# A recurrent attention loop: copies go from VectorE to GpSimd and ScalarE, two softmaxes behind the next query copy, and a load into the step

## The chip, the cores and the metric

The kernel runs on one core of a Trainium2 chip. A core has a matrix engine (TensorE, PE in the profile; its weight loads are PEld), VectorE (DVE), ScalarE (ACT), GpSimd (POOL), SyncE (SP, used here to start transfers) and 16 DMA engines that all transfers share. Each engine takes its instructions in the order in which the program gives them, and an instruction that has to wait holds up the ones behind it on that engine. The metric is the time of one execution in microseconds (us) of device time.

## The reference: what is computed

Two independent results lie side by side in the output. The first is a long convolution by FFT (1024 columns of 2048 rows); the change doesn't touch it. The second is a transformer layer with a memory that recurs over 64 segments of 32 rows:

```
mem = mem0                                   # 8 rows of 1024
for s in range(64):
    h = concat([mem, x[32 s : 32 s + 32]])   # 40 rows
    q, k, v = h Wq, h Wk, h Wv               # 32 heads of 128
    p = softmax(mask(q k^T * 128**-0.5))
    o = sum over heads of (p v) Wo           # 40 rows of 1024
    mem = o[:8];  out[32 s : 32 s + 32] = o[8:]
```

Segment s + 1 needs the 8 memory rows of segment s, so the 64 steps follow one another. A step uses all of Wq, Wk, Wv and Wo.

## The kernel before, in words

**Ahead of the loop.** The FFT convolution runs, and meanwhile everything that doesn't depend on the recurrence is computed for all segments: queries, keys and values of the last 8 rows of each segment (`QKBd`, `VBd` in DRAM). A step then works on 32 rows (8 of memory, 24 of x) and adds those 8 from the stored values.

**Weights.** They are cut into pairs of 512 KB. Most lie in SBUF for good (`Wqk`, `Wv`, `Wo`, `Wearly`); 17 pairs a step are read from DRAM through a ring of five buffers (`wring`, L713, started by SP), and two more are parked in PSUM and copied into ring buffers by ScalarE and VectorE (L719, L720). A ring buffer's next load starts when the matmuls that read it are done (`done`, which calls `place`).

**A step.** The 32 heads go in four units u0 to u3 of 8 heads. The order is written out by hand: a manual schedule puts each engine's instructions in the order of the Python calls in the loop over `s` (L906 on), and no scheduler moves them. The functions are:

- `qk_part` (L753): queries and keys of a unit, accumulated in PSUM over 8 weight pairs. `qk_out` (L759): ScalarE copies them to `qks`.
- `v_part` (L767), `v_out` (L774): the same for the values of two units, into `vsb`.
- `tr_a` (L780, L788 to L790): TensorE transposes `qks`; GpSimd puts the stored keys (`qkb`) and ScalarE the transposed queries and keys into `QK`.
- `scores` (L810 to L825): TensorE writes mask plus products into `S` in PSUM; VectorE takes the row maximum and subtracts it.
- `softmax` (L831 to L842): GpSimd clears part of `P`, ScalarE writes two exponentials into it, VectorE sums, inverts, multiplies and transposes it in place.
- `blocks` (L844 to L852): four copies of 32 partitions by 160 elements from `P` into the block-diagonal `PB`; a letter for each says which engine (D VectorE, P GpSimd, A ScalarE).
- `pv` (L859 to L867): TensorE multiplies `PB` with `vsb` and with the stored values `VB`; ScalarE copies the 32-row part to `OT`, VectorE the 8-row part to `OL`; after u3 GpSimd starts the store of `OL`.
- `wo` (L874): output projection into `Y`. Then `Y` is copied to `Y_sb` (L985), transposed into the next step's `hT` (L893, L894), and stored by four GpSimd DMAs (L989). `load_vb` (L804) starts the 64 KB load of `VB`, on GpSimd's queue.

**Buffers that tie things together.** `qks` and `QK` share one buffer; so do `P` and `Y_sb`. `PB`, `VB` and `OL` are single. The PSUM buffer `ts` is one for `tp` (the transposes), `S` and the tail's transposes: the next transposes wait until the exponentials have read `S`.

**Who waits for whom in `scores`.** The matmul at L816 reads both parts of `QK`, GpSimd's and ScalarE's, and all of TensorE's later work is queued behind it.

Of the kernel before, what the change touches and what calls it, by code (L numbers as in the profile page):

```python
# [21 lines left out]
def fused_kernel(ctx: ExitStack, tc, q, k, v, shift_k, ssm_k, ssm_D, outa, x, mem0, Wq, Wk, Wv, Wo, outb, n_seg):  # L22
# [11 lines left out]
    nc = tc.nc  # L34
    S, D = 2048, 1024
# [672 lines left out]
    def place():  # L708

        if todo:  # L710
            key = todo.pop(0)
            t = ring.tile([128, 2, 1024], BF, tag="wring", name="wring")
            nc.sync.dma_start(t[:], Wst[key])  # L713
            placed.setdefault(key, []).append(t[:])

    def unpark():
        while to_copy:
            key, t = to_copy.pop(0)
            nc.scalar.copy(t[:, 0, :], park[key][0][:])  # L719
            nc.vector.tensor_copy(t[:, 1, :], park[key][1][:])  # L720

    def pair(key):
        return res[key][:, :, :] if key in res else placed[key].pop(0)

    def done(key):
        if key in res:
            return
        if key in PARKED:
            t = ring.tile([128, 2, 1024], BF, tag="wring", name="wring")
            placed[PARKED[key]] = [t[:]]  # L730
            to_copy.append((PARKED[key], t))
        else:
            place()
# [23 lines left out]
    def qk_out(u):  # L757
        u.qks = act.tile([128, 512], BF, tag="qks", name="qks")
        nc.scalar.copy(u.qks[:], u.qk[:])  # L759

    def v_part(G_, kcs):
        if kcs[0] == 0:
            vacc[0] = ps_a.tile([128, 512], F32, tag="a", name="vacc")
        for kc in kcs:
            w = pair(("v", G_, kc))
            for c in range(4):
                nc.tensor.matmul(vacc[0][32 * c:32 * c + 32, :].rearrange("p (n x) -> p n x", n=2), lhsT=hT[:, kc, :],  # L767
                                 rhs=w[:, :, c * 256:(c + 1) * 256], start=(kc == 0), stop=(kc == 7),
                                 tile_position=(0, 32 * c))
            done(("v", G_, kc))  # L770

    def v_out():
        v = act.tile([128, 2, 256], BF, tag="vsb", name="vsb")
        nc.scalar.copy(v[:].rearrange("p n x -> p (n x)"), vacc[0][:])  # L774
        return v
# [16 lines left out]
    def load_b(s):  # L792
        qkb = act.tile([128, 4, 128], BF, tag="qkb", name="qkb")
        nc.sync.dma_start(qkb[:], QKBd[:, :, s * 128:(s + 1) * 128].rearrange("g e x -> e g x"))
        return qkb

    def new_u(g):
        u = G()
        u.g = g
        u.qkb = qkb[:, g, :]  # L800
        return u

    def load_vb(s):
        nc.gpsimd.dma_start(VB[:], VBd[:, :, s].rearrange("c g r x -> (c g) r x"))  # L804
# [23 lines left out]
    def softmax(u, S):  # L828
        P = act.tile([128, 2, 2, 2, 32], BF, tag="P", name="P")
        k0 = 8 * u.g  # L830
        nc.gpsimd.memset(P[:, 1], 0.0)  # L831
        Sv = S[:].rearrange("p (a i) k -> p i a k", a=2)
        nc.scalar.activation(P[:, 0], Sv[:, :, :, 0:32], ACT.Exp, scale=scale)  # L833
        nc.scalar.activation(P[:, 1, :, :, k0:k0 + 8], Sv[:, :, :, 32:40], ACT.Exp, scale=scale)  # L834
        sm = act.tile([128, 4], F32, tag="sm", name="sm")
        Pv = P[:].rearrange("p b i a k -> p b (i a) k")
        nc.vector.tensor_reduce(out=sm[:], in_=Pv.rearrange("p b x k -> p x b k"), op=ALU.add, axis=AX.XY)  # L837
        nc.vector.reciprocal(sm[:], sm[:])
        nc.vector.tensor_tensor(out=Pv, in0=Pv, in1=sm[:].unsqueeze(1).unsqueeze(3).to_broadcast([128, 2, 4, 32]),
                                op=ALU.mult)  # L840
        Pf = P[:].rearrange("p b i a k -> p (b i a k)")
        nc.vector.transpose(out=Pf, in_=Pf)  # L842
        u.PT = P[:].rearrange("p b i a q -> p (b i) (a q)")

    def blocks(u, by):
        for c in range(4):
            r = slice(32 * c, 32 * c + 32)
            to, src = PB[r, :, c, :], u.PT[r, :, 0:40]
            if by[c] == "A":
                nc.scalar.copy(to, src)  # L850
            else:
                (nc.vector if by[c] == "D" else nc.gpsimd).tensor_copy(to, src)  # L852

    def pv(u, s):
        ot = ps_a.tile([128, 512], F32, tag="a", name="otacc")
        for i in range(2):
            o = ot[:, 160 * i:160 * i + 160]
            for kb, w in enumerate((u.v[:, u.g % 2, :], VB[:])):
                nc.tensor.matmul(o, lhsT=w[:, i * 128:(i + 1) * 128], rhs=PB[:, 2 * kb + i].rearrange("p c q -> p (c q)"),  # L859
                                 start=(kb == 0), stop=(kb == 1))  # L860
        u.OT = act2.tile([128, 8, 32], BF, tag="OT", name="OT")
        ov = ot[:, 0:320].rearrange("e (i c q) -> e i c q", i=2, c=4)
        nc.scalar.copy(u.OT[:].rearrange("e (c i) q -> e i c q", i=2), ov[:, :, :, 0:32])  # L863
        to = OL[:] if s + 1 < n_seg else OLs[:, s]
        nc.vector.tensor_copy(to[:, 8 * u.g:8 * u.g + 8, :].rearrange("e (c i) r -> e i c r", i=2), ov[:, :, :, 32:40])
        if u.g == 3 and s + 1 < n_seg:
            nc.gpsimd.dma_start(OLd[s], OL[:].rearrange("e h r -> e (h r)"))  # L867

# [31 lines left out]

    for _ in range(RING):
        place()
    load_vb(0)
    qkb = load_b(0)
    n_o = [key for key in resident if key[0] == "o" and key not in n_o]
    hT = new_hT()  # L906
# [1 line left out]
    for s in range(n_seg):  # L908
        last = s + 1 == n_seg
        def first_loads(g):  # L910
            for key in (n_o[3 * g:3 * g + 3] if s == 0 else ()):
                for n in range(2):
                    res_half(key, n)

        first_loads(0)
        us = [new_u(g) for g in range(4)]
        u0, u1, u2, u3 = us
        qk_part(u0, range(0, 4))
        unpark()
        qk_part(u0, range(4, 8))  # L920
        qk_out(u0)
        v_part(0, range(0, 4))
        tr_a(u0)
        unpark()
        first_loads(1)
        qk_part(u1, range(0, 4))
        S = scores(u0)
        softmax(u0, S)
        blocks(u0, "DDDD")
        qk_part(u1, range(4, 8))  # L930
        qk_out(u1)
        v_part(0, range(4, 8))
        tr_a(u1)
        u0.v = u1.v = v_out()
        first_loads(2)
        qk_part(u2, range(0, 4))
        S = scores(u1)
        softmax(u1, S)
        if last:
            spare = [key for key in resident if key[0] != "o" and key[1] < 1 + (key[0] == "qk") and key not in early]  # L940
            for key, at in zip([key for key in streamed if key[0] == "o"], spare):
                nc.sync.dma_start(res[at][:], Wst[key])
                res[key] = res[at]
        qk_part(u2, range(4, 8))
        qk_out(u2)
        pv(u0, s)
        blocks(u1, "DDDD")
        first_loads(3)
        qk_part(u3, range(0, 2))
        tr_a(u2)  # L950
        qk_part(u3, range(2, 6))
        S = scores(u2)
        softmax(u2, S)
        qk_part(u3, range(6, 8))
        qk_out(u3)
        v_part(1, range(0, 1))
        pv(u1, s)
        blocks(u2, "DDDD")
        v_part(1, range(1, 2))
        tr_a(u3)  # L960
        v_part(1, range(2, 5))
        S = scores(u3)
        if not last:
            H = load_h(s + 1)
            qkb = load_b(s + 1)
        softmax(u3, S)
        v_part(1, range(5, 8))
        u2.v = u3.v = v_out()
        Y = ps_a.tile([128, 512], F32, tag="a", name="yacc")
        wo(u0, Y)  # L970
        if last:
            for s0, s1 in ((0, 32), (32, s)):
                nc.sync.dma_start(OLs[:, s0:s1].rearrange("e s h r -> e s (h r)"),
                                  OLd[s0:s1].rearrange("s e x -> e s x"))
        pv(u2, s)
        blocks(u3, "DDAA")
        wo(u1, Y)
        wo(u2, Y)
        pv(u3, s)
        if not last:  # L980
            hT = new_hT()
            h_rows(H, hT, 8)
        wo(u3, Y)
        Y_sb = act.tile([128, 256], BF, tag="P", name="Y_sb")
        nc.scalar.copy(Y_sb[:], Y[:, 0:256])  # L985
        if not last:
            fill_mem(hT, Y_sb)
        for dq in range(4):
            nc.gpsimd.dma_start(outb[32 * s:32 * s + 24, dq * 256:(dq + 1) * 256], Y_sb[32 * dq + 8:32 * dq + 32, :])  # L989
        if not last:  # L990
            load_vb(s + 1)

    pp.close()
    ps_l = cw_.enter_context(tc.tile_pool(name="b_ps_l", bufs=2, space=PSUM))
# [85 lines left out]
```

## Time and profile before

| | us |
|---|---|
| median of three runs | 2148.98 |
| the three runs | 2133.83, 2148.98, 2156.17 |
| the profiled execution's own time | 2154.46 |
| its span, from the first to the last instruction | 2152.6 |
| copies of `Y` to `Y_sb` (L985), one a step | 64 |
| PE busy / DVE / ACT / POOL, of the span | 1720.4 / 1117.8 / 921.1 / 419.9 |

The loop takes up about three quarters of the span, from some 430 us on; a short tail (projection of the last 8 rows of all segments, L1003) follows after 2089 us. In the profile's rows, "out<-in" names the tile written and the tiles read, "128x64 bf16" is partitions by elements, "x256" is a count, the figures after the bar are total busy us and mean ns of one, and the last ones are the idle time of that engine just before, with what ended it. In the timeline, the first column is the start in us from the span's start and the second the duration; "x4" rows are several instructions merged.

### The profile page before, as it was taken

The numbers are of one execution on the slowest core, as the hardware profiler recorded it, in microseconds if no ns is written. First come the engines' busy times: TensorE is split into PE (matmuls) and PEld (weight loads), VectorE is DVE, ScalarE is ACT, GpSimd is POOL, SyncE is SP. The second block draws the span as 40 slices with busy tenths as digits, with TensorE's granted clock in tenths as the row PEclk, the third lists the DMA queues.
The fourth block names the chain that finished last, engine by engine and source line by source line (L and its number), as shares of the span: only waits on it lengthen the run. The fifth ranks groups of instructions, "written<-read, shape, count | busy, mean of one in ns | idle before, by whom it ended". The sixth has DMA issues, their size and how long they took to land. (4 is left out here: it accounts for less than half of the span.)

```text
span 2152.6 us, 74044 instructions
## 1 busy us (share of the span) xinstructions
PE 1720.4 (80%) x30514; PEld 895.9 (42%) x30514; DVE 1117.8 (52%) x3364; ACT 921.1 (43%) x2282; POOL 419.9 (20%) x1023
## 2 busy tenths in 40 slices
PE   4788987777887887788788888888888878788879
PEld 2332232334443444444444444444444444444448
DVE  6895842245554555555455555555555545555530
ACT  4546741134444444444444444444444444444430
POOL 4003630011111111111111221111111111221110
PEclk8999999889999999999999999999999999999999
DMA  7798969699999999999999999999999999999990
GB/s 238 287 337 312 360 236 355 215 364 360 364 374 323 363 372 368 354 354 352 337 368 369 373 352 372 369 364 365 361 354 367 363 346 375 366 369 371 367 321 22
DMA packets 267375, 728.63 MB, mean 338 GB/s; under 512 B 64751, under 2 KB 75903, under 8 KB 266525
## 3 DMA queue, kind: packets, MB, share of 16 engines
q1 hardware_dynamic: 241294, 687.24, 86.9%
q0 software_dynamic: 15520, 22.06, 3.3%
q10 hardware_dynamic: 10224, 14.62, 1.9%
q8 instruction: 239, 3.92, 0.7%
q14 instruction: 98, 0.80, 0.1%
HBM read 673.52 MB, written 56.56 MB: 339 GB/s over the span
## 5 line engine op out<-in xcount | busy, mean ns | idle before, releaser
L753 PE MATMUL qkacc<-Wqk,hT 128*32 128x512 bf16 x4096 | 339.5, 384 | 0.0
L753 PEld LDWEIGHTS <-hT 128*32 128x32 bf16 x8192 | 185.9, 96 | 241.9 <-issue 92.1
L874 PEld LDWEIGHTS <-OT 128*32 128x32 bf16 x8192 | 210.2, 96 | 108.9 <-issue 59.2
L874 PE MATMUL yacc<-Wo,OT 128*32 128x256 bf16 x5632 | 237.1, 274 | 16.7 <-ACT OT L863 14.7
L753 PE MATMUL qkacc<-wring,hT 128*32 128x512 bf16 x2048 | 207.5, 394 | 32.8 <-DMA wring<-Wstqk 26.5
L767 PE MATMUL vacc<-wring,hT 128*32 128x512 bf16 x1536 | 143.0, 387 | 100.2 <-DMA wring<-in_B_Wv_dram 98.4
L720 DVE COPY wring<-park 128x1024 bf16<-128x1024 bf16 x128 | 88.6, 692 | 242.3 <-PE vacc L767 164.0
L767 PE MATMUL vacc<-Wv,hT 128*32 128x512 bf16 x2560 | 209.8, 382 | 0.0
L767 PEld LDWEIGHTS <-hT 128*32 128x32 bf16 x4096 | 111.3, 95 | 226.4 <-issue 152.4
L833 ACT ACTIVATE P<-S 128x128 bf16<-128x128 f32 x256 | 71.1, 278 | 314.0 <-DVE S L825 233.5
L789 ACT COPY QK<-tp 128x256 bf16<-128x256 bf16 x256 | 95.4, 373 | 237.2 <-PE tp L780 237.2
L788 POOL COPY QK<-qkb 128x64 bf16<-128x64 bf16 x256 | 61.4, 240 | 652.9 <-PE tp L780 487.3
L753 PE MATMUL qkacc<-Wearly,hT 128*32 128x512 bf16 x2048 | 166.4, 403 | 18.5 <-DVE hT L894 17.9
L852 DVE COPY PB<-P 32x160 bf16<-32x160 bf16 x896 | 173.7, 194 | 10.6
L837 DVE TENSOR_REDUCE sm<-P 128x4 f32<-128x256 bf16 x256 | 107.5, 420 | 130.3 <-ACT P L834 130.3
L719 ACT COPY wring<-park 128x1024 bf16<-128x1024 bf16 x128 | 130.7, 1021 | 103.8 <-PE qkacc L753 100.8
L759 ACT CAST qks<-qkacc 128x512 bf16<-128x512 f32 x256 | 150.8, 589 | 28.8 <-PE qkacc L753 23.3
L874 PE MATMUL yacc<-wring,OT 128*32 128x256 bf16 x2520 | 126.4, 274 | 36.2 <-DMA wring<-Wsto 35.2
L863 ACT CAST OT<-otacc 128x256 bf16<-128x256 f32 x256 | 98.4, 384 | 126.8 <-PE otacc L859 126.8
L989 POOL DMA_DIRECT2D out_dram<-Y_sb x256 | 129.1, 511 | 89.9 <-ACT Y_sb L985 87.9
L824 DVE TENSOR_REDUCE mx<-S 128x4 f32<-128x160 f32 x256 | 83.2, 325 | 107.3 <-PE S L821 102.4
L780 PE MATMUL tp<-ident,qks 128*128 128x128 bf16 x1024 | 102.1, 222 | 42.6 <-ACT qks L759 39.3
(216 smaller groups left out, 2827.1 us busy)
## 6 DMA issues: line engine op xcount, KB each, us to landing
wring<-Wstqk SPq DMA_DIRECT2D x448, 512.0 KB, 6.3
wring<-in_B_Wv_dram SPq DMA_DIRECT2D x320, 512.0 KB, 6.7
wring<-Wsto SPq DMA_DIRECT2D x315, 512.0 KB, 6.0
SK<-s_sb SPq DMA_DIRECT2D x8, 1024.0 KB, 7.0
SU<-s_sb SPq DMA_DIRECT2D x8, 1024.0 KB, 6.7
QKBd<-stq ACTq DMA_DIRECT2D x4, 2048.0 KB, 10.9
Kg<-SK SPq DMA_DIRECT2D x16, 512.0 KB, 6.9
Ug<-SU SPq DMA_DIRECT2D x16, 512.0 KB, 7.5
```

Of the source, the lines that this page charges most:

```text
L719: nc.scalar.copy(t[:, 0, :], park[key][0][:])
L720: nc.vector.tensor_copy(t[:, 1, :], park[key][1][:])
L753: nc.tensor.matmul(u.qk[p0:p0 + 32, :], lhsT=hT[:, kc, :], rhs=w[:, t, c2 * 512:(c2 + 1) * 512], start=(kc == 0), stop=(kc == 7), tile_pos ...
L759: nc.scalar.copy(u.qks[:], u.qk[:])
L767: nc.tensor.matmul(vacc[0][32 * c:32 * c + 32, :].rearrange("p (n x) -> p n x", n=2), lhsT=hT[:, kc, :], rhs=w[:, :, c * 256:(c + 1) * 256 ...
L780: nc.tensor.transpose(tp[:, j * 128:(j + 1) * 128], src[:, j * 128:(j + 1) * 128], ident[:])
L789: nc.scalar.copy(u.QT.rearrange("e (c j) r -> e c j r", c=2), tv[:, 0])
L837: nc.vector.tensor_reduce(out=sm[:], in_=Pv.rearrange("p b x k -> p x b k"), op=ALU.add, axis=AX.XY)
L852: (nc.vector if by[c] == "D" else nc.gpsimd).tensor_copy(to, src)
L863: nc.scalar.copy(u.OT[:].rearrange("e (c i) q -> e i c q", i=2), ov[:, :, :, 0:32])
L874: nc.tensor.matmul(Y[32 * dq:32 * dq + 32, 0:256], lhsT=u.OT[:, hh, 0:32], rhs=w[:, hh % 2, dq * 256:(dq + 1) * 256], start=(u.g == 0 and ...
L989: nc.gpsimd.dma_start(outb[32 * s:32 * s + 24, dq * 256:(dq + 1) * 256], Y_sb[32 * dq + 8:32 * dq + 32, :])
```

## The change

Five edits in the loop, and nothing else:

- the `OL` copy in `pv` goes from VectorE to ScalarE, for all four units;
- `blocks` of u0, u1 and u2 goes from "DDDD" to "DDPP": two of the four copies go from VectorE to GpSimd (u3 stays "DDAA");
- `softmax` of u0 and u1 is called behind `qk_part(…, 4..8)` and `qk_out` of the next unit; `blocks(u0)` moves with it, while `blocks(u1)` stays behind `pv(u0)`;
- the copy of `Y` to `Y_sb` is split in halves, ScalarE the first 128 columns, VectorE the second;
- `load_vb` goes from the end of the step before (and from ahead of the loop) to a place behind `tr_a(u0)` in the step itself.

```
-        nc.vector.tensor_copy(to[:, 8 * u.g:8 * u.g + 8, :].rearrange("e (c i) r -> e i c r", i=2), ov[:, :, :, 32:40])
+        nc.scalar.copy(to[:, 8 * u.g:8 * u.g + 8, :].rearrange("e (c i) r -> e i c r", i=2), ov[:, :, :, 32:40])
...
-    load_vb(0)
...
         tr_a(u0)
         unpark()
+        load_vb(s)
         first_loads(1)
         qk_part(u1, range(0, 4))
         S = scores(u0)
-        softmax(u0, S)
-        blocks(u0, "DDDD")
         qk_part(u1, range(4, 8))
         qk_out(u1)
+        softmax(u0, S)
+        blocks(u0, "DDPP")
         v_part(0, range(4, 8))
         tr_a(u1)
         u0.v = u1.v = v_out()
         first_loads(2)
         qk_part(u2, range(0, 4))
         S = scores(u1)
-        softmax(u1, S)
...
         qk_part(u2, range(4, 8))
         qk_out(u2)
+        softmax(u1, S)
         pv(u0, s)
-        blocks(u1, "DDDD")
+        blocks(u1, "DDPP")
         first_loads(3)
         qk_part(u3, range(0, 2))
         tr_a(u2)
         qk_part(u3, range(2, 6))
         S = scores(u2)
         softmax(u2, S)
         qk_part(u3, range(6, 8))
         qk_out(u3)
         v_part(1, range(0, 1))
         pv(u1, s)
-        blocks(u2, "DDDD")
+        blocks(u2, "DDPP")
         v_part(1, range(1, 2))
         tr_a(u3)
...
-        nc.scalar.copy(Y_sb[:], Y[:, 0:256])
+        nc.scalar.copy(Y_sb[:, 0:128], Y[:, 0:128])
+        nc.vector.tensor_copy(Y_sb[:, 128:256], Y[:, 128:256])
...
-        if not last:
-            load_vb(s + 1)
```

More of the change, by code (lines that the diff above doesn't have):

```diff
@@ L864, in pv @@
         to = OL[:] if s + 1 < n_seg else OLs[:, s]
-        nc.vector.tensor_copy(to[:, 8 * u.g:8 * u.g + 8, :].rearrange("e (c i) r -> e i c r", i=2), ov[:, :, :, 32:40])
+        nc.scalar.copy(to[:, 8 * u.g:8 * u.g + 8, :].rearrange("e (c i) r -> e i c r", i=2), ov[:, :, :, 32:40])
         if u.g == 3 and s + 1 < n_seg:
@@ L902, in fused_kernel @@
         place()
-    load_vb(0)
     qkb = load_b(0)
@@ L924, in fused_kernel @@
         unpark()
+        load_vb(s)
         first_loads(1)
@@ L927, in fused_kernel @@
         S = scores(u0)
-        softmax(u0, S)
-        blocks(u0, "DDDD")
         qk_part(u1, range(4, 8))
         qk_out(u1)
+        softmax(u0, S)
+        blocks(u0, "DDPP")
         v_part(0, range(4, 8))
@@ L937, in fused_kernel @@
         S = scores(u1)
-        softmax(u1, S)
         if last:
@@ L945, in fused_kernel @@
         qk_out(u2)
+        softmax(u1, S)
         pv(u0, s)
-        blocks(u1, "DDDD")
+        blocks(u1, "DDPP")
         first_loads(3)
@@ L957, in fused_kernel @@
         pv(u1, s)
-        blocks(u2, "DDDD")
+        blocks(u2, "DDPP")
         v_part(1, range(1, 2))
@@ L984, in fused_kernel @@
         Y_sb = act.tile([128, 256], BF, tag="P", name="Y_sb")
-        nc.scalar.copy(Y_sb[:], Y[:, 0:256])
+        nc.scalar.copy(Y_sb[:, 0:128], Y[:, 0:128])
+        nc.vector.tensor_copy(Y_sb[:, 128:256], Y[:, 128:256])
         if not last:
@@ L989, in fused_kernel @@
             nc.gpsimd.dma_start(outb[32 * s:32 * s + 24, dq * 256:(dq + 1) * 256], Y_sb[32 * dq + 8:32 * dq + 32, :])
-        if not last:
-            load_vb(s + 1)
     pp.close()
```

## The prediction

> **What bounds the kernel now.** I first read the page's slices and costliest groups, then a table by stretches, then the timeline of one step.
>
> From the page, the DMA slices and the groups that wait for weights or matter to the change:
>
> ```profile
> span 2152.6 us, 74044 instructions
> ...
> DMA  7798969699999999999999999999999999999990
> ...
> L753 PE MATMUL qkacc<-wring,hT 128*32 128x512 bf16 x2048 | 207.5, 394 | 32.8 <-DMA wring<-Wstqk 26.5
> L767 PE MATMUL vacc<-wring,hT 128*32 128x512 bf16 x1536 | 143.0, 387 | 100.2 <-DMA wring<-in_B_Wv_dram 98.4
> ...
> L852 DVE COPY PB<-P 32x160 bf16<-32x160 bf16 x896 | 173.7, 194 | 10.6
> ...
> L874 PE MATMUL yacc<-wring,OT 128*32 128x256 bf16 x2520 | 126.4, 274 | 36.2 <-DMA wring<-Wsto 35.2
> ```
>
> In the table by stretches, one row over 55 steps of the loop (PE, PEld, DVE, ACT, POOL busy us, then the granted clock, DMA share, GB/s):
>
> ```profile
> 609.00:2032.00 1423.00, 1152.09 (x23996) 608.49 (x23984) 738.41 (x2530) 625.05 (x1705) 269.55 (x771) 0.99 0.98 362
> ```
>
> The transfers are the bound: a step takes 25.87 us (1423/55) with the DMA engines at 0.98. But TensorE isn't far behind: it waits for streamed weights 32.8 + 100.2 + 36.2 = 169.2 us in 64 steps, 2.64 us a step. So at most 2% (0.5 us a step) is to be gained while the same bytes move, and a delay of TensorE of a few us a step is not covered.
>
> The timeline, from the first unit's exponential to the fourth's, shows the hand-over that the change touches:
>
> ```profile
> 1218.86 0.28 ACT L833 ACTIVATE P<-S 128x128 bf16<-128x128 f32 x1 [0.51 <-PE qkacc L753]
> ...
> 1219.12 0.59 ACT L759 CAST qks<-qkacc 128x512 bf16<-128x512 f32 x1
> ...
> 1220.37 0.24 POOL L788 COPY QK<-qkb 128x64 bf16<-128x64 bf16 x1 [2.06 <-PE tp L780]
> 1220.86 0.81 DVE L852 COPY PB<-P 32x160 bf16<-32x160 bf16 x4
> 1221.08 0.22 PE L816 MATMUL S<-QK 128*32 128x40 bf16 x8
> 1222.56 0.28 ACT L833 ACTIVATE P<-S 128x128 bf16<-128x128 f32 x1 [1.12 <-DVE S L825]
> 1224.56 0.81 DVE L852 COPY PB<-P 32x160 bf16<-32x160 bf16 x4
> 1224.73 0.22 PE L816 MATMUL S<-QK 128*32 128x40 bf16 x8
> 1226.26 0.28 ACT L833 ACTIVATE P<-S 128x128 bf16<-128x128 f32 x1 [1.67 <-DVE S L825]
> 1228.27 0.81 DVE L852 COPY PB<-P 32x160 bf16<-32x160 bf16 x4
> 1228.42 0.23 PE L816 MATMUL S<-QK 128*32 128x40 bf16 x8
> 1229.91 0.28 ACT L833 ACTIVATE P<-S 128x128 bf16<-128x128 f32 x1 [1.61 <-DVE S L825]
> ```
>
> Here GpSimd's key copy for u1 (L788, 1220.37) runs ahead of u0's block copies (1220.86), and u1's scores (L816) start 0.22 us after those, not behind them. GpSimd is idle for 2 us before L788. So today units overlap: the scores of unit u+1 don't wait for the softmax of unit u.
>
> **The change part by part.**
>
> *Block copies on GpSimd.* In each step 6 copies of 32x160 leave VectorE (6 x 194 ns = 1.16 us of its time) and go to GpSimd. In the changed program GpSimd's order in a step is: L788 for u0, `VB` load, clearing and two block copies for u0, L788 for u1, clearing and two block copies for u1, L788 for u2, and so on. The block copies wait for the end of softmax of their unit, and L788 of the next unit is queued right behind them. Behind that L788 waits L816 on TensorE, and behind it everything. This is the term that I expect to decide.
>
> Price of a GpSimd block copy: none is in the trace. The nearest rows are L788 itself (128x64, 240 ns), and GpSimd's copy of 32x544 at L419 (636 ns, the median of most of its groups). Between these two, by elements, 160 come to 0.24 + 96/480 x 0.40 = 0.32 us; bounds 0.24 and 0.64. I take 0.32, since L788 is the nearer row. Two of them: 0.64 us.
>
> Contention with VectorE: the trace has L788 under VectorE's block copies at 1865.74 with 0.30 us, and under its multiplication of two SBUF tensors (L839) at 1013.07 with 0.43 us, against 0.24 alone. I add 0.06 us a unit; the upper bound is the two VectorE block copies that start at the same moment, 0.39 us. The Trainium skill ("SBUF — State Buffer", SBUF: two separate sides) says that VectorE in a two-port mode and GpSimd share a port pair as an exclusive lock on which the loser fully blocks. The two rows agree in kind; by that rule the pair would cost nearer to 0.39 than to 0.06, and it speaks against the change.
>
> *Softmax of u0 and u1 behind the next query copy.* Two clearings (205 ns each, GpSimd), four exponentials and eight VectorE instructions move behind `qk_out`. ScalarE then does L759 first: the exponential of u0 starts when u1's accumulation has ended (1219.02 in the timeline), plus 0.05 for the hand-over and 0.52 from start to next start on ScalarE, at 1219.59, not 1218.86. What is gained: `tr_a` can't be held by an exponential ahead of the copy; but TensorE's transposes need both (`S` and `tp` share a PSUM buffer), so they wait for the same two ScalarE pieces in the other order. In the trace the waits of u1's and u2's transposes come to 0.1 us a step each. I cost the gain at nothing beyond the retiming below.
>
> *The retiming.* Hand-overs from the timeline: exponential to block copies 2.00 us (three units agree: 1218.86 to 1220.86, 1222.56 to 1224.56, 1226.26 to 1228.27); L788 0.24; hand-over to L816 0.08; from L816 to the end of `S` 0.27, to the maximum 0.08, to the subtraction 0.43, to the exponential 0.42, so 1.20 where VectorE is free. For u1 the exponential is behind L759: L816 to the end of u2's accumulation 1.21 (1221.08 to 1222.29), 0.05, 0.52, so 1.78.
>
> - u0's exponential 1219.59. GpSimd done with L788 for u1, L816: + 2.00 + 0.64 + 0.06 + 0.24 + 0.08 = 1222.61 (was 1221.08: +1.53).
> - u1's exponential + 1.78 = 1224.39. L816 of u2 + 3.02 = 1227.41 (was 1224.73: +2.68).
> - u2's exponential + 1.20 = 1228.61. L816 of u3 + 3.02 = 1231.63 (was 1228.42: +3.21).
> - u3's exponential + 1.20 = 1232.83 (was 1229.91: +2.92).
>
> The last is 0.29 less than L816's delay because VectorE is rid of `OL` and two block copies (it reached the maximum of u3 0.46 us after `S`). Behind u3's exponential are the `vsb` copy, `pv(u2)` and the tail, so 2.92 us a step is what the path grows by, if nothing absorbs it.
>
> *What absorbs it.* Counting TensorE's waits for weights by their position over 58 steps of the trace: about 0.6 us a step lie inside the stretch that is stretched (0.31 at the third wait of the values, 0.12 in the second half's values, 0.2 in the queries), and vanish there. Some 1.9 lie in the output projection and at the start of the next step. Of these, only what the DMA engines get ahead during the stall can vanish. They don't get far: a ring of five buffers is full after its loads have landed, and in the trace the last load of a step (`Wsto`, issued when v's last streamed pair is used) already has only some 0.5 us of other loads in front of it (2.3 us from issue to first byte against 1.8 for the least of the 17). I take 0.6. So 2.92 - 1.2 = 1.7 us a step; bounds 2.92 - 2.64 = 0.3 and 2.92.
>
> *`OL` on ScalarE.* Four copies of 128x64 leave VectorE (197 ns) and cost ScalarE about 0.2 us each (between 128x32 at 192 and 128x256 at 384 ns). Behind them on ScalarE wait L789 for u2 and u3 and `blocks(u3)`. The retiming puts `OL` of u0 at its end when u2's transposes end, so nothing is late; cover gone, up to 0.2 us a unit.
>
> *`Y_sb` in halves.* 373 ns becomes two pieces side by side of about 280 (ScalarE 128x128: 278; VectorE between 192 for 64 and 351 for 192 elements), -0.09 us a step, hidden by the values' weights, which TensorE waits for right after. Cost nothing; bounds -0.09 and +0.1 for a second hand-over.
>
> *`VB` load.* It moves past four GpSimd DMA issues of the tail into the step, behind L788 of u0 (1216.91): issue 0.56, landing 5.2 (median of the DMA issues), so 1217.2 + 5.2 = 1222.4 or up to 1224.1 (landing 6.9 at most). `pv(u0)` starts at 1222.24 today, so it would be 0.2 us late, but the stall above moves it to about 1223.8. Behind the issue on GpSimd is the clearing for u0, which waits until 1218.1 for the store of `Y_sb` anyway. Nothing; 0.2 to 1.9 us a step if the stall isn't there.
>
> Sum: 64 x 1.7 = 109 us. The profiled execution of 2154.5 us would become 2263; the median of the runs is 5.5 us lower, 2149 + 109 = **2258 us**.
>
> **The rivals.**
>
> *The weights cover it (no change).* If TensorE's later waits for weights shrink by all they have, 0.3 us a step is left: 2149 + 64 x 0.3 = 2168, 0.9% more. For it: DMA share 0.98. Against: the ring is only five deep, and what isn't issued during the stall isn't made up. Chance 0.13.
>
> *Little is absorbed, or GpSimd is slower.* 2.92 x 64 = 187, so 2336; with copies of 0.64 us another 3 x 0.64 = 1.9 us a step and up to 2460. For it: DMA at 0.98 can't run faster later. Chance 0.14. The lock taken in full adds 3 x 0.33 = 1.0 us a step: 2258 + 63 = 2321; for it the two rows of 0.30 and 0.43, against it that the former is only 0.06. Chance 0.08.
>
> *Faster.* The relief of VectorE and ScalarE is what counts, and GpSimd's copies are done before L788 is needed. Place: u3's maximum, 0.46 us earlier, u2's 0.41 (L824 today follows the block copies), 0.09 in the tail, 0.2 at the transposes: 1.16, of which the DMA engines leave 0.5 us a step, 2149 - 32 = 2117. It decides if L788 of the next unit isn't behind the block copies' wait, that is if block copies would have to start 1.5 us earlier than in the retiming. Against it: the order of GpSimd's queue, and GpSimd's clearing of `P`, which today ends its wait only with VectorE's block copies. Chance 0.07.
>
> **How the numbers follow.** Forecast 0.58, with its own range 2190 to 2310; no change 0.13; the two dearer cases 0.22; faster 0.07. The range from 2165 to 2345 leaves out the faster case, about half of the case of no change and a third of the dearest. A change of 1% is what a measurement of this kernel can tell from none; slower by over 1% (above 2170): 0.58 + 0.22 = 0.80; within 1% 0.13; faster 0.07.
>
> **What would show it.** In the profile after: L788 of u1 to u3 right behind two GpSimd block copies, with L816 waiting for it (POOL as releaser of PE's L816, 64 x 3 times, together over 150 us); GpSimd block copies of about 0.32 us; four exponentials spaced about 4.8, 4.2 and 4.2 us rather than 3.7; DMA share about 0.92; TensorE's waits for weights down from 169 to about 90 us. Wrong it would be if L816 doesn't wait for POOL, or if the step's length stays near 25.9 us although it does.

## The result, and the profile after

| | before | after |
|---|---|---|
| median, us (6 runs each) | 2135.97 | 2315.70 |
| all runs, us | 2133.83 to 2156.17 | 2313.29 to 2325.97 |
| ratio, 95% interval | | 1.0813 [1.0776, 1.0851] |
| profiled execution, span | 2152.6 | 2315.9 |

The change makes the kernel 8.1% slower: 174 us by the ratio, 2.7 us in each of 64 steps (the two medians lie 180 us apart). That lies in the predicted range (2165 to 2345) and in the predicted direction, but the likeliest time was 2258; what was measured lies nearer to the rival in which little is absorbed (2336).

From the page of the changed kernel and its groups of PE, the waits for weights, as shown of before, and the two rows that are new:

```profile
L852 POOL COPY PB<-P 32x160 bf16<-32x160 bf16 x384 | 121.1, 315 | 699.0 <-DVE P L842 312.4
...
L753 PE MATMUL qkacc<-wring,hT 128*32 128x512 bf16 x2048 | 208.2, 392 | 31.4 <-DMA wring<-Wstqk 26.3
L767 PE MATMUL vacc<-wring,hT 128*32 128x512 bf16 x1536 | 143.2, 387 | 104.0 <-DMA wring<-in_B_Wv_dram 103.2
...
L816 PE MATMUL S<-QK 128*32 128x40 bf16 x2048 | 58.9, 185 | 200.6 <-POOL QK L788 200.6
```

```profile
L874 PE MATMUL yacc<-wring,OT 128*32 128x256 bf16 x2520 | 125.0, 274 | 6.5 <-DMA wring<-Wsto 6.2
```

The row of L816 in the kernel before:

```profile
L816 PE MATMUL S<-QK 128*32 128x40 bf16 x2048 | 57.5, 181 | 0.9 <-POOL QK L788 0.9
```

TensorE's score matmuls (L816), which waited 0.9 us for GpSimd in the whole kernel before, now wait 200.6 us for its key copy: 3.1 us a step. The waits for streamed weights have hardly moved: 31.4 + 104.0 + 6.5 = 141.9 us against 169.2.

In the table by stretches, 1530 us of the loop (columns as before):

```profile
660.00:2190.00 1530.00, 1137.35 (x23406) 608.71 (x23401) 665.84 (x1992) 625.61 (x1883) 350.32 (x1072) 0.99 0.92 328
```

The DMA engines went from 0.98 to 0.92 busy at the same granted clock of 0.99: transfers wait for instructions now.

The timeline of one step after, with the same instructions as shown of before:

```profile
1200.11 0.58 ACT L759 CAST qks<-qkacc 128x512 bf16<-128x512 f32 x1 [0.79 <-PE qkacc L753]
1200.59 0.28 ACT L833 ACTIVATE P<-S 128x128 bf16<-128x128 f32 x1
...
1201.79 0.40 PE L780 MATMUL tp<-ident,qks 128*128 128x128 bf16 x4
...
1202.61 0.46 DVE L852 COPY PB<-P 32x160 bf16<-32x160 bf16 x2
1202.70 0.67 POOL L852 COPY PB<-P 32x160 bf16<-32x160 bf16 x2 [3.61 <-DVE P L842]
...
1203.43 0.24 POOL L788 COPY QK<-qkb 128x64 bf16<-128x64 bf16 x1
...
1203.72 0.23 PE L816 MATMUL S<-QK 128*32 128x40 bf16 x8
...
1205.65 0.28 ACT L833 ACTIVATE P<-S 128x128 bf16<-128x128 f32 x1
...
1207.79 0.67 POOL L852 COPY PB<-P 32x160 bf16<-32x160 bf16 x2 [3.98 <-DVE P L842]
1208.52 0.23 POOL L788 COPY QK<-qkb 128x64 bf16<-128x64 bf16 x1
1208.81 0.23 PE L816 MATMUL S<-QK 128*32 128x40 bf16 x8 [1.30 <-POOL QK L788]
1210.04 0.28 ACT L833 ACTIVATE P<-S 128x128 bf16<-128x128 f32 x1 [2.84 <-DVE S L825]
```

Read it downwards: query copy, then the exponential of u0, then VectorE's chain, two block copies on GpSimd, only then the key copy of u1 and its scores. In the kernel before, the key copy follows the transposes of its unit (L780) by some 0.2 us. Here u1's transposes end at 1202.19 (1201.79 + 0.40) and the key copy starts at 1203.43, 1.24 us later: GpSimd waits another 0.5 us for u0's softmax and then makes the two block copies. Most of its 3.61 us of idle time lies ahead of those transposes. Over 58 steps the key copies of u1 to u3 start 1.92, 2.05 and 1.57 us after their transposes, against 0.16 or 0.17 in the kernel before. Exponential to exponential is 5.06 us (u0 to u1) and 4.39 (u1 to u2), where it was 3.70 and 3.70.

### The profile page after: what moved, and what is told of

Read it like the earlier page. It is cut to its first block, busy times and chain, and to the rows that moved or that the text cites. A ratio compares the mean times of both kernels' runs of the same rounds, so it can differ in the third digit from the quotient of the medians.

```text
span 2315.9 us, 74046 instructions
## 1 busy us (share of the span) xinstructions
PE 1736.9 (75%) x30514; PEld 914.7 (39%) x30514; DVE 1050.9 (45%) x2788; ACT 939.4 (41%) x2538; POOL 525.9 (23%) x1407
## 4 chain that ended last, share of the span: by engine, by line
DMA 32%; PE 27%; DVE 15%; ACT 11%; issue 8%; POOL 5%; SPq 1%; ACTq 0%; POOLq 0%; DVEq 0%
DMA wring<-in_B_Wv_dram 15%; DMA wring<-Wstqk 8%; PE qkacc L753 6%; PE yacc L874 5%; POOL PB L852 3%; DVE P L842 3%; DVE P L839 3%; DVE sm L837 3%; PE pl L1002 2%; ACT vsb L774 2%; ACT P L833 2%; POOL QK L788 2%; PE S L816 2%; DVE S L825 2%; DVE mx L824 2%
## 5 line engine op out<-in xcount | busy, mean ns | idle before, releaser
L852 POOL COPY PB<-P 32x160 bf16<-32x160 bf16 x384 | 121.1, 315 | 699.0 <-DVE P L842 312.4
L753 PE MATMUL qkacc<-wring,hT 128*32 128x512 bf16 x2048 | 208.2, 392 | 31.4 <-DMA wring<-Wstqk 26.3
L767 PE MATMUL vacc<-wring,hT 128*32 128x512 bf16 x1536 | 143.2, 387 | 104.0 <-DMA wring<-in_B_Wv_dram 103.2
L816 PE MATMUL S<-QK 128*32 128x40 bf16 x2048 | 58.9, 185 | 200.6 <-POOL QK L788 200.6
L816 PEld LDWEIGHTS <-QK 128*32 128x32 bf16 x2048 | 53.5, 97 | 233.7 <-issue 230.7
L780 PE MATMUL tp<-ident,qks 128*128 128x128 bf16 x1024 | 101.1, 221 | 45.7 <-ACT qks L759 30.6
```

Source lines behind the costliest of these rows:

```text
L753: nc.tensor.matmul(u.qk[p0:p0 + 32, :], lhsT=hT[:, kc, :], rhs=w[:, t, c2 * 512:(c2 + 1) * 512], start=(kc == 0), stop=(kc == 7), tile_pos ...
L780: nc.tensor.transpose(tp[:, j * 128:(j + 1) * 128], src[:, j * 128:(j + 1) * 128], ident[:])
L816: nc.tensor.matmul(S[32 * c:32 * c + 32, i, :], lhsT=u.QT[:, hh, :], rhs=u.KT[:, hh, :], start=False, stop=False, tile_position=(0, 32 * c))
```

## The experiments

Ratios are to runs of the kernel before on the same chip, with 95% intervals.

### The block copies: place or engine?

**e1_blocks_back** and **e3_blocks_behind** start from the changed kernel.

```
e1:  -        blocks(u0, "DDPP")        +        blocks(u0, "DDDD")        (u1, u2 the same)
```

> The changed kernel with the six block copies back on VectorE (DDDD for u0, u1, u2), the rest of the change kept. Queue theory (the key copy L788 of the next unit stands behind the GpSimd block copies of a unit that isn't through softmax yet): the waits of L816 for POOL go from 201 us to under 10, and the time to 2120 to 2155 us, within 1% of the kernel before (2136). Rival (the softmax calls behind the query copy, or the late VB load, cost the time): it stays above 2220.

Measured: 2182.86 us, 1.0181 [1.0121, 1.0240]. L816 waits 0.8 us for GpSimd. The bulk of the loss is gone, but less than the queue theory said: 1.8% stays, and belongs to the other edits.

```
e3:  -        blocks(u0, "DDPP")
              v_part(0, range(4, 8))
              tr_a(u1)
     +        blocks(u0, "DDPP")                                           (u1, u2 the same)
```

> The changed kernel with the calls of blocks for u0, u1, u2 placed behind tr_a of the next unit: the same six copies on GpSimd, but the key copy L788 ahead of them in GpSimd's queue. Queue theory: the waits of L816 for POOL vanish (under 15 us) and the time is 2115 to 2155 us. Rival (GpSimd's copies are slow, or GpSimd and VectorE block each other at the shared memory): GpSimd still does the same work beside the same VectorE instructions, so the time stays above 2200 us.

Measured: 2170.60 us, 1.0112 [1.0055, 1.0169]; L816 waits 2.2 us for GpSimd. GpSimd still makes the 384 copies, at 322 ns each (315 in the changed kernel). So what cost the time isn't the engine, nor that VectorE and GpSimd work beside each other, which they do here too: it is the place in GpSimd's queue. A rest of 1.1% stays here too, just over the forecast.

**e2_blocks_alone** is the kernel before with "DDPP" for u0, u1 and u2 and nothing else.

> The kernel before with DDPP for u0, u1, u2 and nothing else. Queue theory, with the hand-overs of the retiming and u0's exponential at its old place: L816 at +0.9, +1.5 and +2.1 us against before, u3's exponential +1.8 us, so 64 x 1.8 = 115 us at most: 2215 to 2250 us, less than the whole change's +180 because the softmax move adds 0.7 us (u0) and 0.6 us (u1) to the same chain. Rival (the softmax move is the cause): within 1% of 2136.

Measured: 2248.33 us, 1.0486 [1.0436, 1.0537], so 104 us; L816 waits 128.0 us for GpSimd, 2.0 a step. In the forecast, at its upper part.

**e4_blocks_four** is the changed kernel with "PPPP".

> The changed kernel with PPPP: all four block copies of u0, u1, u2 on GpSimd, so two more copies of 0.315 us in front of L788 for each of three units. Queue theory: each step grows by 3 x 0.63 = 1.9 us, 64 x 1.9 = 121 us, to 2410 to 2440 us. Rival (the transfers absorb a delay, as the prediction took for 1.2 us a step): 2316 plus at most 60. Rival (VectorE and GpSimd block each other): no VectorE block copy runs beside them any more, GpSimd's copies get shorter than 0.315 us.

Measured: 2456.18 us, 1.1456 [1.1390, 1.1522], 138 us over the change by the two ratios, against 121 forecast; L816 waits 296.8 us. GpSimd's copies take 315 ns, as with VectorE's beside them. But they don't follow each other at once: in the timeline four take 1.38 us and two 0.67, so that two more cost 0.71 us a unit and not 0.63. Over 58 steps L816 comes 3.87 us after the exponential, 0.71 later than in the changed kernel, and 64 x 3 x 0.71 = 136 us is nearly all that was measured. So the forecast priced the copy too low; the dose counts fully, and nothing absorbs a further delay.

### The other edits, one at a time, on the kernel before

**e5_softmax_alone**: only the two softmax calls (with their block copies, all on VectorE) behind the query copy.

> The kernel before with only the softmax calls of u0 and u1 behind the next query copy (their block copies stay on VectorE, DDDD, at the places of the change). After the first four runs there are two theories for the 1 to 2% that stay when the block copies are back or out of the way. Softmax theory: the exponentials of u0 and u1 start 0.6 to 0.7 us later, so the block copies of u1 end later, pv(u1) waits for them, and the maximum of u2, behind them on VectorE, comes later: 0.3 to 0.6 us a step, 2155 to 2175 us. Load theory (the late VB load costs it): within 0.5% of the kernel before.

Measured: 2183.43 us, 1.0177 [1.0149, 1.0205], 38 us, 0.6 a step: the upper end of the softmax theory's price, and far outside the load theory's. The timeline of e5, from u2's scores to u3's transposes:

```profile
1205.98 0.21 PE L821 MATMUL S<-QK,qkb 128*8 128x40 bf16 x8
...
1206.26 0.81 DVE L852 COPY PB<-P 32x160 bf16<-32x160 bf16 x4
...
1207.11 0.32 DVE L824 TENSOR_REDUCE mx<-S 128x4 f32<-128x160 f32 x1
...
1207.96 0.28 ACT L833 ACTIVATE P<-S 128x128 bf16<-128x128 f32 x1 [2.17 <-DVE S L825]
...
1208.21 0.59 ACT L759 CAST qks<-qkacc 128x512 bf16<-128x512 f32 x1
...
1208.86 0.40 PE L780 MATMUL tp<-ident,qks 128*128 128x128 bf16 x4 [0.67 <-ACT qks L759]
```

u2's `S` is complete at 1206.19 (1205.98 + 0.21), but its maximum starts at 1207.11, 0.92 us later (0.41 in the step shown of before; over 58 steps 0.88 against 0.28), because VectorE first makes u1's late block copies (0.81 us from 1206.26). The exponential of u2 and, behind it on ScalarE, the query copy of u3 are late by that, and TensorE waits for the copy. Counted over 58 steps, TensorE's wait at u3's transposes grows from 0.49 to 0.89 us a step, and `pv(u1)`, which didn't wait, waits 0.22 for u1's block copies.

**e11_softmax_u1**: of these two moves only u1's.

```
-        softmax(u1, S)
         ...
         qk_part(u2, range(4, 8))
         qk_out(u2)
+        softmax(u1, S)
         pv(u0, s)
```

> The kernel before with only u1's softmax behind the query copy of u2; u0's stays. Theory (u1's is the costly one: its exponentials come 0.3 to 0.7 us later, so its four block copies on VectorE end later, and u2's maximum, its exponential and the query copy of u3 behind that on ScalarE): most of the 38 us of both together, 2155 to 2180. Rival (u0's delay is handed on): under 10 us, 2130 to 2150.

Measured: 2169.00 us, 1.0107 [1.0062, 1.0153], 23 us, with the same two waits (0.89 and 0.21 us a step). u1's move is the larger part; by difference u0's costs some 0.7%, so u0's delay isn't handed on without cost either.

**e6_vb_alone**: only the `VB` load moved.

> The kernel before with only the VB load moved into the step. Load theory: pv(u0), which the stall no longer pushes back, finds VB late in most steps, by 0.2 to 0.7 us: 2150 to 2180 us. Softmax theory: late in a few steps only, 2130 to 2148 us, within 0.5% of the kernel before.

Measured: 2147.28 us, 1.0009 [0.9979, 1.0040]: no measurable difference. `pv(u0)` waits in 6 of 58 steps, 0.11 us a step on average.

**e7_copies_alone**: only `OL` on ScalarE and `Y_sb` in halves.

> The kernel before with only the OL copies on ScalarE and Y_sb in halves. VectorE reaches the maxima of u2 and u3 0.2 us earlier and the tail is 0.1 us shorter; the transfers leave at most 0.5 us a step: 2110 to 2136 us. Rival (a second hand-over in the tail and a longer ScalarE queue eat it): 2136 to 2150.

Measured: 2155.89 us, 1.0035 [1.0010, 1.0060]: a little slower, as the rival said. From the groups of VectorE in e7:

```profile
L986 DVE CAST Y_sb<-yacc 128x128 bf16<-128x128 f32 x64 | 18.7, 292 | 104.6 <-ACT Y_sb L985 104.6
```

The halves don't run side by side. VectorE's waits for ScalarE's in all 64 steps, so 266 and then 292 ns stand where one copy of 373 was. The changed kernel shows the same wait, 100.0 us in all.

### Does anything absorb the delay?

**e9_light_before** and **e10_light_after** are the two kernels with fewer transfers:

```
+    LIGHT = {("v", 0, 0), ("v", 0, 5), ("v", 1, 1), ("v", 1, 5)}
-    todo = [key for s in range(n_seg) for key in streamed if key[0] != "o" or s < n_seg - 1]
+    todo = [key for s in range(n_seg) for key in streamed if key not in LIGHT and (key[0] != "o" or s < n_seg - 1)]
     def pair(key):
+        if key in LIGHT:
+            return res["v", 0, 2]
```

> The kernel before with 4 of the 17 streamed weight pairs a step left out: v(0,0), v(0,5), v(1,1) and v(1,5) are not loaded, and their matmuls read the resident pair v(0,2) instead, so part of the values is computed with other weights; all instructions of the engines stay. Both theories: the transfers no longer bound it and TensorE's waits for the values' weights go from 100 us to under 30: 2020 to 2090 us. The run is the base for the next one.

> The changed kernel with the same 4 pairs left out, and the same resident pair read instead. What it costs over the light kernel before is the growth of the path with nothing for the transfers to absorb. Theory A (the path grew by the predicted 2.9 us a step and the transfers absorbed nearly nothing of it in the full kernels): 64 x 2.9 = 186, so 175 to 200 us over the light kernel before. Theory B (the path grew by more, and the transfers did absorb the predicted 1.2 us): 64 x (2.75 + 1.2) = 253, so 235 to 270 us over it.

Measured: 2008.24 us (0.9350 [0.9305, 0.9396]), a little under the forecast, and 2189.59 us (1.0189 [1.0140, 1.0238]). The table by stretches, first of e9, then of e10:

```profile
660.00:2000.00 1340.00, 1119.37 (x24462) 636.92 (x24466) 724.74 (x2486) 615.72 (x1678) 264.77 (x759) 1.00 0.85 295
```

```profile
660.00:2000.00 1340.00, 1037.85 (x21897) 567.52 (x21898) 620.82 (x1854) 588.53 (x1755) 330.05 (x1006) 0.99 0.78 272
```

With the DMA engines at 0.85 and 0.78 and waits for weights down to 31 and 24 us in all, the change costs 2189.59 - 2008.24 = 181 us, 2.83 us a step. In the full kernels it costs 174 (166 to 182 by the interval). So the growth of the path was priced nearly right (2.92), and if it is the same in the full kernels, the transfers absorbed about 0.1 us a step of it: theory A.

### A version that beats both

**e8_best** is the kernel before with the two copies of e7 and the block copies of e3.

> The kernel before with the OL copies on ScalarE, Y_sb in halves, and two block copies of u0, u1, u2 on GpSimd, called behind tr_a of the next unit so that the key copy is ahead of them; softmax and VB load stay where they were. Queue theory: no wait of L816 for POOL, the maxima of u2 and u3 0.4 us earlier, 2100 to 2135 us. If GpSimd's work itself costs time, slower than the copies alone by over 0.5%.

Measured: 2145.05 us, 0.9965 [0.9935, 0.9996]. The wait is gone (L816 waits 1.9 us for GpSimd), and it is 0.7% faster than the copies alone (e7), so GpSimd's part isn't what costs; but the gain is less than was forecast.

**e12_blocks_behind_alone** leaves the copies of e7 out.

```
-        blocks(u0, "DDDD")
...
         tr_a(u1)
+        blocks(u0, "DDPP")                                                (u1, u2 the same)
```

> The kernel before with DDPP for u0, u1, u2, called behind tr_a of the next unit, and nothing else. Queue theory: no wait for POOL at L816, and u2's and u3's maxima come up to 0.4 us earlier: 0.3 to 1.0% faster than before, 2115 to 2140 us. Rival (GpSimd's part costs as much as VectorE gains): within 0.2% of before.

Measured: 2134.00 us, 0.9929 [0.9900, 0.9957], the fastest version that loads all weights: 0.7% faster than the kernel before. The timeline of e12 around u1's key copy:

```profile
1231.32 0.29 POOL L788 COPY QK<-qkb 128x64 bf16<-128x64 bf16 x1 [2.92 <-PE tp L780]
1231.67 0.67 POOL L852 COPY PB<-P 32x160 bf16<-32x160 bf16 x2
```

The key copy is through before GpSimd turns to the blocks, and L816 waits 2.4 us for it in the whole kernel. TensorE's wait at u3's transposes falls from 0.49 to 0.35 us a step and that at `pv(u2)` from 0.53 to 0.28. e8, which has e7's two copies on top, gains half as much, but the two intervals overlap.

## Why the prediction was right, and where it was not

**The deciding mechanism: shown.** Key copies behind block copies in GpSimd's queue, L816 behind them. Four runs carry it: with the same work on GpSimd in another place (e3, e12) the wait is gone, alone (e2) it costs 104 us, and with twice the copies (e4) 138 more.

**The retiming: right in its sum.** GpSimd's copy was taken at 0.32 us and takes 0.315. The stretches between exponentials were forecast at 4.80 and 4.22 us and are 5.06 and 4.39 in the step shown; L816 for u2 and u3 comes 3.16 and 3.15 us after the exponential (3.02 forecast). Over 58 steps the three spacings are 5.01, 4.39 and 4.31 us. In the kernel before they were 3.98, 3.90 and 3.66, so the step on which the retiming was done (3.70, 3.70, 3.65) was a quick one. The growth of 2.92 us a step is 2.83 where the transfers are out of the way, but that the sums agree so well is in part luck: in the light pair u0's exponential comes only 0.11 us later in its step (0.73 forecast), the three spacings grow by 1.22, 0.69 and 0.66 (1.10, 0.52 and 0.57 forecast), and what follows u3's exponential grows by 0.17.

**What absorbs it: the step that failed.** The term was 1.2 us a step, half of it waits for weights inside the stretch that grows, half of it waits behind that stretch; TensorE's waits for weights were to fall from 169 to about 90 us. The light pair puts the term at about 0.1 (7 us, with the change's interval of 8 us either way, so it may be nothing), and TensorE's waits for weights fell by 0.43 us a step (169.2 to 141.9 us in 64 steps). Between these two it stays open, but either is about a third of 1.2 or less: 64 x 0.8 to 1.1 is 50 to 70 us, which is why 2258 was too low. It would have been lower still from the median of six runs: 2149, from which it starts, was that of three, 13 us higher.

Where the waits went, counted over 58 steps of each trace: from u0's exponential to u3's it is 11.54 us before and 13.71 after (11.14 and 13.71 in the light pair), so 0.40 of the first 0.6 did vanish; the waits at the third and later pairs of the values fell by 0.27 a step. Behind u3's exponential the step got shorter, 7.20 to 6.46 us, and the waits of the projection went as expected (36.2 to 6.5 us in all, 0.46 a step). But ahead of u0's exponential the step got 1.19 us longer and not 0.73: the first two waits of the values, early in a step, grew from 0.96 to 1.33. The output projection, no longer held up, uses its streamed pairs in quicker succession, and each use starts a load for the next step's start: the load of v(0,3) is issued 0.66 us after the one before it (1.09 in the kernel before) and lands 7.6 us after its issue (7.3). So the burst of loads and the wait behind it moved on with the stall. That this is the reason is read from the two traces; no run changed it alone. The rival in which the weights cover everything is ruled out by the same numbers; "little is absorbed" was the right case, at 2.7 instead of 2.92 us.

**Softmax behind the query copy: priced in the chain, too low by itself.** The prediction saw its 0.7 and 0.6 us in the chain with GpSimd, and costed it at nothing beyond. Alone it costs 38 us (e5), by a way that the prediction didn't name: late block copies on VectorE hold up the next unit's maximum. The single edits add up to 38 + 2 + 8 + 104 = 152 us of 174, but the rest, 22 us, is hardly more than the five intervals leave open (17 us either way together), and the sum hides that e5's way is closed in the changed kernel: over 58 steps the maximum of u2 starts 0.07 us after `S`. There the moved softmax lengthens the chain that GpSimd's copies make: u0's exponential to u1's is 5.01 us against 4.41 in e2. The block copies cost 135 us with the other edits in place (1.0813 - 1.0181, e1) and 104 alone.

**`VB`: right**, and the cover needn't even be there: without the stall it was to cost 0.2 to 1.9 us a step, and the wait is 0.11. **`OL`**: 238 ns on ScalarE (0.2 forecast). **`Y_sb` in halves: wrong sign.** The second hand-over was bounded at +0.1; one half after the other makes the copies 0.19 us longer (0.266 + 0.292 - 0.373).

**VectorE beside GpSimd.** From the start of VectorE's block copies to the key copy it is 0.82 and 0.79 us in the step shown, where the forecast had 0.70 (0.64 for GpSimd's pair, 0.06 for contention); GpSimd's pair takes 0.67 and starts 0.06 to 0.09 after VectorE's. GpSimd's first and VectorE's second copy of the step shown, singly:

```profile
1202.70 0.31 POOL L852 COPY PB<-P 32x160 bf16<-32x160 bf16 x1 [3.61 <-DVE P L842]
1202.81 0.26 DVE L852 COPY PB<-P 32x160 bf16<-32x160 bf16 x1
```

VectorE's second copy ends 0.05 to 0.06 us after GpSimd's first in 187 of the 192 pairs of the kernel, whether the two pairs had started 0.06 or 0.10 us apart; it takes 220 to 260 ns then, and 192 without GpSimd's beside it. So it waits for GpSimd's. That agrees with the lock of the Trainium skill ("SBUF — State Buffer", SBUF: two separate sides), on which the loser fully blocks, provided that VectorE's copies run in a two-port mode, which no run here tells. But the loser is VectorE, by 0.03 to 0.07 us: GpSimd's copies take 315 ns with VectorE's beside them and without (e4), so the rival's 0.33 us a unit doesn't come.

**Faster** was ruled out for the change as it is, but its mechanism exists: once the key copy is ahead, the relief of VectorE is worth 0.7% (e12).

## What to carry to other kernels

When an operation goes to an idle engine, look at what stands behind it in that engine's queue and when its input comes: here two copies of 0.3 us a unit on an engine that was 80% idle cost 104 us, because a key copy stood behind them that was ready before they were, and the same copies placed behind that key copy gain 0.7%. A DMA share of 0.98 was no cushion here: when one stretch of the step grew, the waits for weights behind it fell, but those at the start of the next step grew, and a pair of kernels with fewer transfers shows how little was absorbed in all. Splitting a copy over two engines helps only if the program lets the halves run side by side; one row of the waits tells.

## What the runs showed that was not expected

- The stall barely changes what the transfers cost: leaving 4 of 17 loads out takes 6.5% off the kernel before (1 to 0.9350) and 6.2% of it off the changed one (1.0813 to 1.0189), 140 and 134 us, although the DMA engines were 0.98 busy in the one and 0.92 in the other.
- Where GpSimd's and VectorE's copies of 32x160 run beside each other, it is VectorE's second that waits, and briefly: 234 ns on average against 192, while GpSimd's take 309 to 370.
- In e4 TensorE's granted clock was 0.93 in the loop, against 0.99 in the changed kernel, though TensorE was busy for no larger a share of it (73% against 74%). What e4 has more of is long waits: TensorE stood idle for over 1.5 us at a time 93 times between 660 and 1990 us, against 10 times. Whether that is the cause, no run shows.
